# Linear attention and ELU feed-forward on one core: one matmul slice and one VectorE sum reordered at the end of the kernel

## The chip, the core and the metric

The kernel runs on one core of a Trainium2 chip. The core has a matrix engine (TensorE, PE in the profile), two element-wise engines that can read the accumulators in PSUM (VectorE or DVE, ScalarE or ACT), a third one that works on SBUF only here (GpSimd or POOL), and a queue engine that issues most stores (SyncE or SP). Each engine works through its own instructions in the order in which they were written; engines wait for each other by semaphores. The metric is the device time of one execution in microseconds (us); lower is better.

## What is computed

The reference runs a decaying linear attention (4 batches, 8 heads, 768 positions, head size 64) and feeds its output, as 3072 tokens of 512 features, through a feed-forward layer with an ELU:

```python
x = attn_out.transpose(0, 2, 1, 3).reshape(B * S, H * D)   # 3072 x 512
h = x @ w_in                                               # 512 x 2048
g = np.where(h > 0.0, h, alpha * (np.exp(np.minimum(h, 0.0)) - 1.0))
return (g @ w_out).astype(np.float32)                      # 2048 x 512
```

The change lies wholly in the second product, `g @ w_out`, for the last tokens.

## The kernel before

**Tiling.** The 3072 tokens are 24 blocks of 128 (`NG = 24`). Blocks 0 to 3 go singly, all others in pairs, named by the first block: 4, 6, ... 22. `mm1` computes one eighth of a pair's `h` at a time (8 matmuls into a PSUM tile `psH`); ScalarE then makes `e = exp(h)` (line 680) and the positive part of `h` in place (line 681). The ELU itself, `g = min(e - 1, max(h, 0))`, is one VectorE operation in `flush` (line 640): it is issued not with its own `mm1`, but by the next `flush`, that is at the beginning of the next `mm1` or of the next step of the second product. `pending` holds what has not been issued yet.

**The second product of the pairs 8 to 22** (`SEVEN`) is done by `mm2_seven` (from line 522) as seven products in place of eight: two blocks of tokens, two halves of the hidden features (`f`) and two halves of the output columns (left `L_`, right `R_`, 256 wide) make a 2 x 2 by 2 x 2 product, and sums of blocks are multiplied. `mm2_seven(g0, i)` issues product m = 3, 4, 5, 2, 1, 7, 6 for i = 0 to 6. Each product is `NFT // 2` = 8 slices, one matmul each (line 551), and slice s reads the g tile `gg` of index s // 2, half s % 2. So slice 7 of a product needs the very last g of its pair, and slices 0 to 6 don't. Products 3 and 4 multiply g itself, 5 and 2 the row sums `fp` (VectorE, line 500), 1 the sums `fe`, 7 and 6 the differences `fd`; for pair 22, `fe` and `fd` are made by GpSimd (line 497, `SHARED[22] = 'ED'`).

**Banks.** A pair uses two PSUM banks of 512 columns. `bank0` takes m3 and, added onto it, m5 in the left half, then m1 and, added onto it, m6 in the right half. `bank1` takes m4 and, added onto it, m2 on the left, and m7 on the right. There are two such banks in all (`sides`); the next pair takes the same two the other way round, so `bank1` of pair 22 is the bank in which m1 and m6 of pair 20 were summed.

**What is read out of the banks**, in order: `keep` copies m3 and m4 to SBUF (ScalarE, line 558), GpSimd adds them to `t` (line 594); `corner` copies m3 + m5 and m4 + m2 to the output tiles `osb` (ScalarE, line 569); GpSimd forms `u = t - corner 0` (line 605) and `s2 = t - corner 1` (written over `t`, line 565); VectorE adds m1 to `u` (also line 565) and then forms the two remaining corners from `u` with m7 and from `s2` with m6 + m1 (line 582, "corner sums" below). The corner sums are not issued at once: `last_of` puts them into the list `later`, and `flush` issues them at its end, behind a g that it has just issued and behind one of the row sums (`slow`) that follow from it. Steps 0 and 1 of `mm2_seven` also empty `later` before they take a bank (lines 530 to 534):

```python
        if i < 2:
            while later:
                later.pop(0)[1]()
            z[f"bank{i}"] = ps.tile(
                [128, DM], FP32, tag=f"psM{sides[i]}", name=f"psM{g0 + i}", bufs=1
            )
```

**Order at the end.** A list of steps is written out by the planner (lines 814 to 823): one step of the second product behind each `mm1` while there are `mm1` left, the rest after them. The last steps are: `mm1` of pair 22 (j = 6), step 5 of pair 20 (m7), `mm1` of pair 22 (j = 7, the last), step 6 of pair 20 (m6), then steps 0 to 6 of pair 22 with nothing between them. In that order, step 6 of pair 20 begins with a `flush`, which issues the last g of pair 22 and its row sum `fp`; the corner sum on m6 of pair 20 is issued at the start of step 0 of pair 22.

**Stores.** Both blocks of pair 20 are stored as a whole (256 KB each), those of pair 22 in four quarters (128 KB), by SP in the order in which they were put on the list `stores` (line 624).

Of the kernel before, what the change touches and what calls it, by code (L numbers as in the profile page):

```python
# [15 lines left out]
def kernel(  # L16
# [11 lines left out]
    nc = tc.nc  # L28
# [7 lines left out]
    NFT = DFF // 128  # L36
    NCB = S // L
    NG = B * NCB
# [22 lines left out]
    LAGU = 13  # L61
    LATE = 4
    MACT = 12
    DELAY = 0
    COMB = nc.gpsimd

# [44 lines left out]
    for w in RAW.split():  # L111
        x = {"q": q, "k": k}[w[0]]
        g0 = int(w[1:])
        raw[w] = asb.tile([128, H, 64], FP32, name=f"raw_{w}", tag=f"raw_{w}")
        (nc.sync if w[0] == "q" else nc.scalar).dma_start(
            out=raw[w][:], in_=x[g0, :, 0:L].rearrange("h p d -> p h d")
# [16 lines left out]
    wi16, wo16, wi_of, wo_of = [], [], {}, {}  # L133
# [67 lines left out]
    def zero_st1(b):  # L201
# [21 lines left out]
        out=ident16[:], in0=row[:], scalar1=pos[:, 0:1], scalar2=None, op0=ALU.is_equal  # L223
    )
    nc.vector.tensor_scalar(
        out=causT[:], in0=row[:], scalar1=pos[:, 0:1], scalar2=None, op0=ALU.is_ge
# [143 lines left out]
    def att_M(g):  # L370
# [9 lines left out]
        stt[g] = tmp  # L380
        if g >= MACT:
            for hp in range(NHP):
# [98 lines left out]
    g2, forms, wf, C_done, seven, slow = {}, {}, {}, set(), {}, []  # L481

    def sums(g0, jj):
        t = g2[(g0, jj)]
        p = msb.tile([128, 2, 2, 128], FP16, tag="g", bufs=24, name=f"fp{g0}_{jj}")
        d = msb.tile([128, 2, 2, 128], FP16, tag="g", bufs=24, name=f"fd{g0}_{jj}")
        e = msb.tile([128, 2, 128], FP16, tag="g", bufs=24, name=f"fe{g0}_{jj}")
        forms[(g0, jj)] = (p, d, e)
        ring["n"] += 3
        todo = []  # L490
        for w, out, in0, in1, op in (
            ("P", p, t[:, :, 0], t[:, :, 1], ALU.add),
            ("E", e, t[:, :, 0, 0], t[:, :, 1, 1], ALU.add),
            ("D", d, t[:, :, :, 1], t[:, :, :, 0], ALU.subtract),
        ):
            if w in SHARED.get(g0, ""):
                nc.gpsimd.tensor_tensor(out=out[:], in0=in0, in1=in1, op=op)  # L497
            else:
                todo.append(
                    lambda out=out, in0=in0, in1=in1, op=op: nc.vector.tensor_tensor(  # L500
                        out=out[:], in0=in0, in1=in1, op=op
                    )
                )
        return todo
# [14 lines left out]
    L_, R_ = slice(0, 256), slice(256, 512)  # L519
    later, sides = [], [0, 1]  # L520

    def mm2_seven(g0, i):
        flush()
        while slow and i in (2, 4, 5):
            slow.pop(0)()
        if i == 0:
            seven[g0] = {}
            sides.reverse()
        z = seven[g0]
        while i == 6 and "w1" not in z:  # L530
            late.pop(0)()
# [5 lines that stand above are left out]
            )  # L537
        m = (3, 4, 5, 2, 1, 7, 6)[i]
        half = L_ if i < 4 else R_
        out = z["bank1" if m in (4, 2, 7) else "bank0"][:, half]  # L540
        for s in range(NFT // 2):
            t = g2[(g0, s // 2)]
            p, d, e = forms[(g0, s // 2)]
            u = s % 2
            lhs = {3: t[:, u, 0, 0, :], 4: t[:, u, 1, 1, :], 1: e[:, u, :], 7: d[:, u, 1, :],
                   6: d[:, u, 0, :], 5: p[:, u, 0, :], 2: p[:, u, 1, :]}[m]
            if m in (5, 2):
                rhs = wo16[s][:, 1, R_] if m == 5 else wo16[s][:, 0, L_]
            else:
                rhs = wf[s][:, (3, 4, 1, 6, 7).index(m), :]  # L550
            nc.tensor.matmul(  # L551
                out, lhsT=lhs, rhs=rhs, start=(s == 0 and m in (3, 4, 1, 7)),
                stop=(s == NFT // 2 - 1), skip_group_check=True,
            )

        def keep(n):
            z[n] = msb.tile([128, 256], FP32, tag=n, bufs=1, name=f"{n}_{g0}")
            nc.scalar.copy(out=z[n][:], in_=out)  # L558

        def comb(n, x, y, op, eng=COMB):  # L560

            z[n] = z[x]
            if eng is nc.vector:
                y = out
            eng.tensor_tensor(out=z[n][:], in0=z[x][:], in1=y, op=op)

        def corner(c, half):
            z[c] = msb.tile([128, DM], FP32, tag="osb512", bufs=4, name=f"osb{g0 + c}")
            nc.scalar.copy(out=z[c][:, half], in_=out)
            if last:  # L570
                store(c, half)

        last = g0 == NG - 2

        def store(c, cols):
            cb, b = divmod(g0 + c, B)
            t0 = b * S + cb * L
            stores.append((out_dram[t0 : t0 + 128, cols], z[c][:, cols]))

        def last_of(c, half, x, op):  # L580
            def one():
                nc.vector.tensor_tensor(out=z[c][:, half], in0=z[x][:], in1=out, op=op)  # L582
                store(c, half if last else slice(0, DM))
                C_done.add(g0 + c)

            later.append([DELAY, one])


        if m == 3:
            keep("m3")  # L590
        elif m == 4:
            keep("m4")
            z["t"] = msb.tile([128, 256], FP32, tag="t", bufs=1, name=f"t_{g0}")
            nc.gpsimd.tensor_tensor(  # L594
                out=z["t"][:], in0=z["m3"][:], in1=z["m4"][:], op=ALU.add
            )
        elif m == 5:
            corner(0, R_)
            z["u"] = msb.tile([128, 256], FP32, tag="u", bufs=1, name=f"u_{g0}")
            if COMB is nc.vector:  # L600
                late.insert(0, lambda: nc.vector.tensor_tensor(
                    out=z["u"][:], in0=z["t"][:], in1=out, op=ALU.subtract
                ))
            else:
                nc.gpsimd.tensor_tensor(
                    out=z["u"][:], in0=z["t"][:], in1=z[0][:, R_], op=ALU.subtract
                )
        elif m == 2:
            corner(1, L_)
            if COMB is nc.vector:  # L610
                late.insert(0, lambda: comb("s2", "t", None, ALU.subtract))
            else:
                comb("s2", "t", z[1][:, L_], ALU.subtract)
        elif m == 1:
            late.insert(0, lambda: comb("w1", "u", None, ALU.add, nc.vector))
        elif m == 7:
            last_of(0, L_, "w1", ALU.subtract)
        else:
            last_of(1, R_, "s2", ALU.add)
# [6 lines left out]
    def flush():  # L626
        while pending:
            g0, j, e, r = pending.pop(0)
            n = GSIZE[g0]
            if g0 in SEVEN:  # L630
                if j % 2 == 0:
                    g2[(g0, j // 2)] = msb.tile(
                        [128, 2, 2, 2, 128], FP16, tag="g2", bufs=8, name=f"gg{g0}_{j}"
                    )
                g = g2[(g0, j // 2)][:, j % 2]
            else:
                g = msb.tile(
                    [128, FB // n, n, 128], FP16, tag="g", bufs=24, name=f"g{g0}_{j}"
                )[:]
            nc.vector.scalar_tensor_tensor(  # L640
                out=g.rearrange("p f c t -> p (f c t)"), in0=e[:], scalar=-1.0, in1=r[:],
                op0=ALU.add, op1=ALU.min,
            )
            for f in range(FB // n):
                for c in range(n):
                    gts[(g0 + c, j * (FB // n) + f)] = g[:, f, c, :]
            if g0 in SEVEN and j % 2 == 1:
                slow.extend(sums(g0, j // 2))
        if late:
            late.pop(0)()  # L650
        if slow and len(late) < 2:
            slow.pop(0)()
        for x in later:
            x[0] -= 1
        while later and later[0][0] <= 0:
            later.pop(0)[1]()
# [136 lines left out]
    for g in range(0, NG, 2):  # L793
        u = place[(GFIRST[g], 0)] - (8 if GSIZE[GFIRST[g]] == 4 and g == GFIRST[g] else 0)
# [19 lines left out]
    for x, (g, j) in enumerate(m1):  # L814
        u = first + x
# [3 lines left out]
        n = 2 if back > LAGU and m2[0][0][0] == "2" else 1  # L819
# [44 lines left out]
```

## Time and profile before

| what | value |
|---|---|
| median of 6 runs | 214.51 us (213.37 to 215.1) |
| profiled execution, its own time | 214.35 us |
| span in its profile | 212.6 us |
| mean granted TensorE clock | 0.997 of full speed |
| TensorE matmuls: sum of busy time, number | 197.0 us, 2224 |
| matmuls of the second product of pairs (line 551), busy | 49.7 us in three groups of 128 (16.8, 16.5, 16.4) |
| TensorE idle ahead of its two waiting matmuls at the end | 0.32 us (for a g) and 0.50 us (for a corner sum) |
| last corner sum, start | 209.29 us |

The span runs from the first to the last instruction of the profiled execution; the time of the execution holds some 1.75 us more. In a timeline each line has the start, the length, the engine, the line of the kernel, the operation, what it writes and reads, the shape, how many of them were merged, and in brackets the idle time of the engine ahead of it with what ended it. The length of a matmul row holds the time in which the last matmul drains, so rows overlap; a sequence of matmuls is read by the starts. The chain of waits is followed back from the last instruction: at each step to what released it, or to the instruction before it on its engine.

### The profile page before, as it was taken

To read this page: it belongs to the slowest core of one execution; us is meant where nothing else is said; L and a number is where in the kernel's file an instruction comes from. 1 tells how busy PE (TensorE), PEld (TensorE's weight loads), DVE (VectorE), ACT (ScalarE), POOL (GpSimd) and SP (SyncE) were. 2 spreads that over 40 slices of the span, in tenths; PEclk is the share of its full clock that TensorE was granted. 3 is DMA by queue.
4 is the path that set the end of the run, shared out by engine and by line. 5 is a ranking of instruction groups with operands and counts; after the bars stand their busy time and mean duration, and the time that the engine had idled before them with its cause. 6 is when DMAs were issued, how large, how long until landed. Compare 5 with 4: busy or idle time off the path is not lost.

```text
span 212.6 us, 5654 instructions
## 1 busy us (share of the span) xinstructions
PE 197.0 (93%) x2224; PEld 157.8 (74%) x2224; DVE 159.0 (75%) x294; ACT 138.0 (65%) x277; POOL 159.9 (75%) x187
## 2 busy tenths in 40 slices
PE   0679999999999999999999999999999999999983
PEld 0458776767676775757887887888988888888862
DVE  3864472589956878899879879879989889885522
ACT  4535764874877675866966967867667667577630
POOL 7999699999999999497999999996361201206961
PEclk9999999999999999999999999999999999999998
DMA  8999999999992030999969969979999611011032
GB/s 91 137 164 185 195 189 186 160 186 185 161 152 76 3 99 4 135 160 150 133 89 160 119 81 158 154 52 153 144 89 172 101 52 49 3 49 49 3 117 80
DMA packets 102122, 24.61 MB, mean 116 GB/s; under 512 B 92624, under 2 KB 99280, under 8 KB 102096
## 3 DMA queue, kind: packets, MB, share of 16 engines
q0 software_dynamic: 79760, 13.50, 82.7%
q1 hardware_dynamic: 22336, 10.76, 26.7%
q8 instruction: 17, 0.28, 0.6%
q14 instruction: 9, 0.07, 0.2%
HBM read 27.27 MB, written 6.29 MB: 158 GB/s over the span
## 4 chain that ended last, share of the span: by engine, by line
PE 74%; ACT 7%; DVE 6%; DMA 6%; POOL 3%; issue 1%; SPq 0%; ACTq 0%; POOLq 0%; DVEq 0%
PE psH L674 34%; PE psM L551 21%; PE psM L699 11%; DMA wi<-in_moe_w_in_dram 3%; ACT e L680 3%; ACT psH L681 3%; PE psS L304 3%; DVE gg L640 2%; PE psO L340 2%; DMA kT<-kn 2%; DVE g L640 2%; PE psO L346 2%; POOL kn L107 1%; PE psT L285 1%; POOL qn L107 1%
## 5 line engine op out<-in xcount | busy, mean ns | idle before, releaser
L674 PE MATMUL psH<-xt,wi 128*128 128x256 f16 (+1 forms) x896 | 101.1, 261 | 3.0 <-DVE gg L640 1.6
L674 PEld LDWEIGHTS <-wi 128*128 128x128 f16 x896 | 79.0, 100 | 18.3 <-issue 4.2
L680 ACT ACTIVATE e<-psH 128x512 f32<-128x512 f32 x96 | 57.3, 597 | 48.2 <-PE psH L674 47.3
L681 ACT ACTIVATE psH<-psH 128x512 f32<-128x512 f32 x96 | 56.9, 593 | 0.0
L640 DVE SCALAR_TENSOR_TENSOR gg<-e,psH 128x512 f16<-128x512 f32 x64 | 43.7, 682 | 16.5 <-ACT psH L681 16.2
L640 DVE SCALAR_TENSOR_TENSOR g<-e,psH 128x512 f16<-128x512 f32 x32 | 21.9, 684 | 17.4 <-ACT psH L681 17.2
L320 DVE TENSOR_TENSOR pp<-psS,mask 128x512 f16<-128x512 f32 x48 | 31.4, 683 | 3.9 <-PE psS L304 3.9
L699 PE MATMUL psM<-wo,g 128*128 128x512 f16 x128 | 32.0, 379 | 0.0
L176 POOL TENSOR_TENSOR kd<-kn,ks 128x512 f16<-128x512 f16 x20 | 21.0, 1052 | 5.0 <-DMA kn<-in_k_dram 5.0
L497 POOL TENSOR_TENSOR fd<-gg 128x512 f16<-128x512 f16 x20 | 24.3, 1217 | 0.1
L517 POOL TENSOR_TENSOR wf<-wo 128x256 f16<-128x256 f16 (+1 forms) x28 | 21.1, 791 | 0.2
L497 POOL TENSOR_TENSOR fe<-gg 128x256 f16<-128x256 f16 x16 | 11.7, 734 | 12.2 <-DVE gg L640 10.9
L594 POOL TENSOR_TENSOR t<-m,m 128x256 f32<-128x256 f32 x8 | 5.9, 737 | 18.3 <-ACT m L558 18.3
L699 PEld LDWEIGHTS <-g 128*128 128x128 f16 x128 | 11.7, 98 | 9.6 <-issue 0.2
L551 PE MATMUL psM<-wf,gg 128*128 128x256 f16 x128 | 16.8, 273 | 0.8 <-DVE osb L582 0.5
L551 PE MATMUL psM<-wo,fp 128*128 128x256 f16 x128 | 16.5, 273 | 0.0
L551 PE MATMUL psM<-wf,fd 128*128 128x256 f16 x128 | 16.4, 273 | 0.0
L107 POOL DMA_DIRECT2D qn<-in_q_dram x13 | 14.8, 1137 | 0.9 <-POOLq L848 0.8
L107 POOL DMA_DIRECT2D kn<-in_k_dram x14 | 15.4, 1099 | 0.0
L107 POOL DMA_DIRECT2D vn<-in_v_dram x14 | 15.3, 1100 | 0.0
L500 DVE TENSOR_TENSOR fp<-gg 128x512 f16<-128x512 f16 x32 | 14.4, 451 | 0.6
L551 PEld LDWEIGHTS <-gg 128*128 128x128 f16 x128 | 12.0, 98 | 3.2 <-issue 0.7
(62 smaller groups left out, 249.8 us busy)
## 6 DMA issues: line engine op xcount, KB each, us to landing
out_dram<-osb SPq DMA_DIRECT2D x22, 256.0 KB, 2.7
kn<-in_k_dram POOLq DMA_DIRECT2D x10, 256.0 KB, 6.2
qn<-in_q_dram POOLq DMA_DIRECT2D x10, 256.0 KB, 5.8
vn<-in_v_dram POOLq DMA_DIRECT2D x10, 256.0 KB, 8.7
wi<-in_moe_w_in_dram POOLq DMA_DIRECT2D x8, 256.0 KB, 8.5
wo<-in_moe_w_out_dram POOLq DMA_DIRECT2D x8, 256.0 KB, 8.9
kn<-in_k_dram POOLq DMA_DIRECT2D x4, 128.0 KB, 4.3
vn<-in_v_dram POOLq DMA_DIRECT2D x4, 128.0 KB, 5.6
```

The source lines that it names most:

```text
L107: nc.gpsimd.dma_start(out=t[:].rearrange("p b h d -> p (b h) d"), in_=src)
L176: nc.gpsimd.tensor_tensor(out=kd[:], in0=of(kg, g), in1=ks[:].unsqueeze(2).broadcast_to([128, H, 64]), op=ALU.mult,)
L320: nc.vector.tensor_tensor(out=P[:], in0=pts[hh][:], in1=mask[:, hh::2, :], op=ALU.mult)
L497: nc.gpsimd.tensor_tensor(out=out[:], in0=in0, in1=in1, op=op)
L500: lambda out=out, in0=in0, in1=in1, op=op: nc.vector.tensor_tensor(out=out[:], in0=in0, in1=in1, op=op)
L517: eng.tensor_tensor(out=out, in0=in0, in1=in1, op=op)
L551: nc.tensor.matmul(out, lhsT=lhs, rhs=rhs, start=(s == 0 and m in (3, 4, 1, 7)), stop=(s == NFT // 2 - 1), skip_group_check=True,)
L640: nc.vector.scalar_tensor_tensor(out=g.rearrange("p f c t -> p (f c t)"), in0=e[:], scalar=-1.0, in1=r[:], op0=ALU.add, op1=ALU.min,)
L674: nc.tensor.matmul(pH[:, f * n * 128 : (f + 1) * n * 128], lhsT=wi16[i][:, kk, w * 128 : (w + 1) * 128], rhs=xg[g0][:, kk, :], start=(kk = ...
L680: nc.scalar.activation(e[:], pH[:], AF.Exp)
L681: nc.scalar.activation(pH[:], pH[:], AF.Relu)
L699: nc.tensor.matmul(psM[g][:, cols], lhsT=gts[(g, j * FB + f)], rhs=wo16[i][:, w, cols], start=first and f == 0, stop=end and f == FB - 1, ...
```

## The change

For the last pair (`last`, pair 22) and the one before it (`NG - 4`, pair 20) three things are ordered otherwise:

- Step 6 of pair 20 no longer begins with a `flush`. The last g of pair 22 is issued by the `flush` of step 0 of pair 22, and that step first issues what is in `later`, the corner sum on m6 of pair 20. So on VectorE the order becomes corner sum, g, `fp`, in place of g, `fp`, corner sum.
- Step 0 of pair 22 issues only slices 0 to 6 of m3 and returns.
- Step 1 issues slices 0 to 2 of m4 (`SPLIT = 3`), then slice 7 of m3, ScalarE's copy of m3, and slices 3 to 7 of m4.

The matmul loop becomes a function `terms(m, slices)`, `keep` takes the number of the product, and `last` is set at the top; for all other pairs the order of the instructions is the same. The numbers of instructions stay the same on each engine.

```diff
+    SPLIT = 3
...
     def mm2_seven(g0, i):
-        flush()
+        last = g0 == NG - 2
+        if last and i == 0:
+            while later:
+                later.pop(0)[1]()
+        if g0 != NG - 4 or i < 6:
+            flush()
...
-        out = z["bank1" if m in (4, 2, 7) else "bank0"][:, half]
-        for s in range(NFT // 2):
...
+        def place_of(m):
+            return z["bank1" if m in (4, 2, 7) else "bank0"][:, half]
+
+        def keep(m):
+            n = f"m{m}"
             z[n] = msb.tile([128, 256], FP32, tag=n, bufs=1, name=f"{n}_{g0}")
-            nc.scalar.copy(out=z[n][:], in_=out)
+            nc.scalar.copy(out=z[n][:], in_=place_of(m))
+
+        def terms(m, slices):
+            for s in slices:
...
+                nc.tensor.matmul(
+                    place_of(m), lhsT=lhs, rhs=rhs,
+                    start=(s == 0 and m in (3, 4, 1, 7)),
+                    stop=(s == NFT // 2 - 1), skip_group_check=True,
+                )
+
+        end = NFT // 2
+        if last and i == 0:
+            terms(3, range(end - 1))
+            return
+        if last and i == 1:
+            terms(4, range(SPLIT))
+            terms(3, [end - 1])
+            keep(3)
+            terms(4, range(SPLIT, end))
+        else:
+            terms(m, range(end))
+        out = place_of(m)
```

More of the change, by code (lines that the diff above doesn't have):

```diff
@@ L539, in mm2_seven @@
         half = L_ if i < 4 else R_
-        out = z["bank1" if m in (4, 2, 7) else "bank0"][:, half]
-        for s in range(NFT // 2):
[L542 to L554, printed above, removed]
@@ L556, in keep @@
-        def keep(n):
-            z[n] = msb.tile([128, 256], FP32, tag=n, bufs=1, name=f"{n}_{g0}")
-            nc.scalar.copy(out=z[n][:], in_=out)
+        def place_of(m):
+            return z["bank1" if m in (4, 2, 7) else "bank0"][:, half]
+        def keep(m):
+            n = f"m{m}"
+            z[n] = msb.tile([128, 256], FP32, tag=n, bufs=1, name=f"{n}_{g0}")
+            nc.scalar.copy(out=z[n][:], in_=place_of(m))
+        def terms(m, slices):
+            for s in slices:
+                t = g2[(g0, s // 2)]
+                p, d, e = forms[(g0, s // 2)]
+                u = s % 2
+                lhs = {3: t[:, u, 0, 0, :], 4: t[:, u, 1, 1, :], 1: e[:, u, :],
+                       7: d[:, u, 1, :], 6: d[:, u, 0, :], 5: p[:, u, 0, :],
+                       2: p[:, u, 1, :]}[m]
+                if m in (5, 2):
+                    rhs = wo16[s][:, 1, R_] if m == 5 else wo16[s][:, 0, L_]
+                else:
+                    rhs = wf[s][:, (3, 4, 1, 6, 7).index(m), :]
+                nc.tensor.matmul(
[3 more added lines that the diff above has]
+                )
@@ L560, in comb @@
+        end = NFT // 2
[7 more added lines that the diff above has]
+            terms(4, range(SPLIT, end))
+        else:
+            terms(m, range(end))
+        out = place_of(m)
         def comb(n, x, y, op, eng=COMB):
@@ L571, in corner @@
                 store(c, half)
-        last = g0 == NG - 2
         def store(c, cols):
@@ L589, in mm2_seven @@
         if m == 3:
-            keep("m3")
+            keep(3)
         elif m == 4:
-            keep("m4")
+            keep(4)
             z["t"] = msb.tile([128, 256], FP32, tag="t", bufs=1, name=f"t_{g0}")
```

## The prediction

> **What bounds the kernel now.** I read the table of engines first, then the chain of waits over the last stretch, then each engine's timeline from 200 us on, because the diff touches only what the two last pairs of token blocks issue after the last `mm1`.
>
> ```profile
> PE 197.0 (93%) x2224; PEld 157.8 (74%) x2224; DVE 159.0 (75%) x294; ACT 138.0 (65%) x277; POOL 159.9 (75%) x187
> ```
>
> TensorE is busy for 93% of the span, so at the end too only what makes TensorE stand still can be won. The chain of waits (start, length, what) ends so:
>
> ```profile
> 201.15 0.60 ACT e L680
> 201.75 0.50 ACT psH L681
> 202.25 0.02 issue
> 202.27 0.70 DVE gg L640
> 202.97 0.05 issue
> 203.01 0.29 PE psM L551
> 203.31 0.03 issue
> 203.33 0.42 DVE osb L582
> 203.76 0.04 issue
> 203.80 5.41 PE psM L551 x48
> ...
> 209.29 0.42 DVE osb L582
> ```
>
> The reader is to see that from 201.15 to 203.80 the chain is twice off TensorE, with one matmul between, and that from 203.80 on it is TensorE alone up to the last corner sum. The timeline of TensorE gives the stalls:
>
> ```profile
> 200.89 1.04 PE L551 MATMUL psM<-wf,fd 128*128 128x256 f16 x8
> 201.76 0.93 PE L551 MATMUL psM<-wf,gg 128*128 128x256 f16 x7
> 203.01 0.28 PE L551 MATMUL psM<-wf,gg 128*128 128x256 f16 x1 [0.32 <-DVE gg L640]
> 203.80 1.03 PE L551 MATMUL psM<-wf,gg 128*128 128x256 f16 x8 [0.50 <-DVE osb L582]
> 204.67 1.91 PE L551 MATMUL psM<-wo,fp 128*128 128x256 f16 x16
> ```
>
> Row one is m6 of pair 20. Row two is seven slices of m3 of pair 22, row three its eighth, which waits for the last g; row four is m4 of pair 22, which waits until pair 20's last corner sum has left the bank; then m5 and m2. Eight matmuls are issued in 0.87 us (204.67 - 203.80), so one takes 0.109 us; the 1.03 and 1.04 in the rows hold the 0.17 us in which the last one drains. Seven slices from 201.76 are issued by 202.53, and the eighth is issued only at 203.01. VectorE's timeline says why m4 waits:
>
> ```profile
> 186.91 0.41 DVE L565 TENSOR_TENSOR u<-u,psM 128x256 f32<-128x256 f32 x1
> 187.24 0.68 DVE L640 SCALAR_TENSOR_TENSOR gg<-e,psH 128x512 f16<-128x512 f32 x1
> ...
> 202.27 0.69 DVE L640 SCALAR_TENSOR_TENSOR gg<-e,psH 128x512 f16<-128x512 f32 x1 [0.73 <-ACT psH L681]
> 202.99 0.43 DVE L500 TENSOR_TENSOR fp<-gg 128x512 f16<-128x512 f16 x1
> 203.33 0.41 DVE L582 TENSOR_TENSOR osb<-t,psM 128x256 f32<-128x256 f32 x1
> ```
>
> The corner sum that frees the bank stands third in VectorE's queue, behind the last g and its row sum `fp`. Its matmuls were done at 201.93 (200.89 + 1.04), and VectorE idled 0.73 us ahead of the g. So the chain's step from TensorE to `osb` at 203.31 is a coincidence of times; the sum waited for its queue.
>
> **The change part by part.** No instruction is added or removed on any engine: it is the same 16 matmuls for m3 and m4, one ScalarE copy of m3, one corner sum, one g, one `fp`, and the same stores. Three things are moved.
>
> *Corner sum ahead of the g.* It can begin 0.09 after m6's end (the corner sums at 208.42 and 209.29 start 0.08 to 0.09 after their matmuls): 201.93 + 0.09 = 202.02, and ends at 202.43. The g's inputs are ready at 202.27, so now it queues behind the sum. Rows two above show a g 0.33 us after the start of a 0.41 us sum (187.24 - 186.91; its ScalarE input was done at 187.02, so the queue held it). That gives 202.02 + 0.33 = 202.35, the g 0.08 late. Bounds: 0 late if the sum hid wholly in the idle 0.73, 0.16 late if the g waited for the sum's whole 0.41; I take 0.08 as its row is the same pair of operations. Behind the late g stand `fp` (its readers, slices 6 and 7 of m5, come 0.65 after m5's start) and GpSimd's `fe` and `fd`, priced below.
>
> The Trainium skill has a rule against putting the sum in front: in "VectorE: DVE Perf Modes", section "The DRAIN you can't avoid", each operation is followed by a flush of about its duration less 266 ns, during which the next can't start. By it, an estimate from that page, the flush of the 0.41 us sum is 0.15, the g would start at 202.58, and the gain worked out here would shrink by 0.23. The rows at 186.91 and 187.24 speak against it.
>
> *Three slices of m4 ahead of m3's eighth.* m4's bank is free when the sum ends; TensorE went on 0.06 after it in the row at 203.80 (203.33 + 0.41 = 203.74), so here at 202.49, just before TensorE gets there at 202.53. Three slices, 3 x 0.109, last to 202.86. The g runs from 202.35 to 203.04 (0.69), and 0.05 later (202.27 + 0.69 = 202.96 to 203.01) m3's eighth slice starts: 203.09. TensorE idles 0.23 here, and m4's other five slices are issued by 203.09 + 6 x 0.109 = 203.75, or 0.1 later if the eighth slice's own weight load, which starts with it, isn't hidden.
>
> *m3's copy inside m4.* m5 adds onto m3 in the same half of the same bank, so m5's first matmul waits for ScalarE's copy of m3. In the old order all eight slices of m4 lay behind that copy; now five do. Before: eighth slice 203.01, copy from 203.39 to 203.76 (0.38 later, 0.37 long). After: 203.09 + 0.38 = 203.47, copy to 203.84, and TensorE goes on 0.05 after a ScalarE copy (`kT` copy from 55.65 for 0.59, matmul at 56.29): 203.89. This new wait covers the weight-load doubt. Its bound from below is 203.81, with the 0.30 from last matmul to copy seen at m4 and m5 (last issue 205.43, copy 205.74). Queued behind it on TensorE are m5 and all that follows. m4's copy ends about 204.4, ahead of m2 at 204.76, so it costs nothing; uncovered it would cost its 0.37.
>
> *Sum.* m5 started at 204.67 and will at 203.89: a gain of 0.78. What follows has to shift as a whole. GpSimd: `fe` 203.11 to 204.02 (m1 wants it after 205.64), `fd` to 205.13 (m7 wants it after 207.1), then t 205.09 to 205.81 (it starts only 0.23 earlier than before, since `fd` is now in front of it, not m4's copy), u to 206.5, s2 to 207.2. VectorE's sum on m1 comes at 206.78, so u is ready 0.28 ahead, and s2 more than 1 us ahead of the last sum. The last corner sum goes from 209.29 to 208.51. The four quarter stores on SP keep their order and spacing; the store of pair 20's second block is issued at about 202.5 and not 203.8, 0.9 after the one in front (0.33 us of issue), so it collides with nothing. The 2.9 us from the last sum to the end of the span stay.
>
> The profiled execution took 214.35 us, 1.75 outside its span of 212.6. With 0.78 off, span 211.8 and time 213.6; the median of the six runs stands 0.16 higher, so 214.51 - 0.78 = 213.7 (-0.36%).
>
> **Range of the forecast itself.** Least: g 0.16 late and nothing won elsewhere, gain 0.70; with the weight load or one more handover of 0.05 to 0.1 showing, 0.6. Most: g on time and the copy 0.30 behind, m5 at 203.73, gain 0.94. That is 213.6 to 213.9.
>
> **The rivals.**
>
> *The split hides nothing; only the bank wait goes.* If the three slices of m4 don't get in front (bank freed late, since there is only 0.04 between 202.49 and 202.53), all of m4 follows m3's eighth: issued by 203.09 + 9 x 0.109 = 204.07, gain 0.60, 213.9. Against it: even 0.2 late, the slices still fit into the 0.23 of idle.
>
> *GpSimd becomes the bound.* It has 0.28 to spare at u. If t, u or the hand-overs from ScalarE slip by 0.6, the sum on m1 is 0.3 late; m6 needs its bank back (0.14 to spare), so 0.2 to 0.3 of the gain is lost: gain 0.5, 214.0. For it: t, u and s2 run now without gaps. Against: their durations were 0.72 to 0.73 in all six rows.
>
> *The corner sum holds the g: slower.* The sum stands at the head of VectorE's queue and waits for m6 of pair 20, for s2 on GpSimd and for the buffer's former store. Each 0.1 by which it starts late holds the g, and with it m3, m4, all of m5 and the end. Break-even is a start 0.78 after 202.02, at 202.80; if it came at 204.0 the time would be 214.51 + 1.2 = 215.7. Against it: m6 is in front on TensorE without a wait, s2 ended at 199.56, and ScalarE wrote the same buffer at 196.92, so the store was over.
>
> *More than the tail.* Nothing ahead of 201 us is moved, so no case gives over 0.94; a median below 213.4 would be scatter: the six runs reach from 213.37 to 215.1.
>
> **How the numbers follow.** Forecast 0.75, the split hiding nothing 0.10, GpSimd 0.08, slower 0.05, more 0.02. A measurement of this kernel tells about 0.5%, or 1.07 us, from no change. The forecast's 0.36% lies inside that, nearer its lower edge; with a scatter of some 0.3 to 0.4 in a median of six runs of this spread, about a third of its weight falls below 213.44, and a little of the smaller gains: faster 0.26. Slower 0.05 from its rival; the same 0.69. The range takes the 213.6 to 213.9 and the scatter of such a median on both sides, and on the upper one the smaller gains: 212.9 to 214.5.
>
> **What would show it.** Right: in VectorE's timeline the corner sum at about 202.0 ahead of the g at about 202.35; on TensorE ten matmuls in a row, a gap near 0.23, six more, then a gap near 0.14 that ends by ScalarE's copy of m3; m5 at about 203.9, last corner sum about 208.5, span 211.8. Wrong: a g later than 202.6, an m5 that follows m4 without a gap, or a wait for GpSimd ahead of the sum on m1.

## The result and the profile after

| | kernel before | changed kernel |
|---|---|---|
| median | 213.71 us (69 runs, 212.76 to 215.1) | 212.96 us (32 runs, 212.07 to 214.1) |
| ratio to before, 95% interval | | 0.9966 [0.9954, 0.9978] |
| span of the profile | 212.6 us | 212.2 us |
| start of pair 20's m6, in the profile | 200.89 us | 201.27 us |
| from there to the start of pair 22's m5 | 3.78 us | 3.00 us |
| from there to the last corner sum | 8.40 us | 7.63 us |

The changed kernel is 0.34% faster, or 0.73 us of 213.71, with an interval of 0.47 to 0.98 us. That is clear of zero and below the 0.5% named in the prediction.

The two profiles can't be compared by their absolute times: 0.38 us are lost ahead of the changed stretch in the changed kernel's profile (201.27 - 200.89), where both kernels issue the same instructions in the same order. So all that follows is read from the start of pair 20's m6. The chain of waits of the changed kernel from 201 us on (start, length, what), its last 8 pieces:

```profile
201.96 0.45 issue
202.40 0.42 DVE osb L608
202.82 0.61 DVE gg L666
203.43 0.05 issue
203.48 5.34 PE psM L567 x46
208.81 0.04 DVEq L608
208.85 0.04 issue
208.90 0.42 DVE osb L608
```

The chain of before came back to TensorE between the g and the corner sum and left it again; this one leaves it once. The sum is now ahead of the g, and the TensorE piece has 46 matmuls (m3's eighth slice, five slices of m4, and 40 of m5 to m6). The timelines of TensorE and VectorE, of the changed kernel:

```profile
201.27 1.04 PE L567 MATMUL psM<-wf,fd 128*128 128x256 f16 x8
202.15 2.16 PE L567 MATMUL psM<-wf,gg 128*128 128x256 f16 x16
204.27 1.91 PE L567 MATMUL psM<-wo,fp 128*128 128x256 f16 x16
```

```profile
202.40 0.42 DVE L608 TENSOR_TENSOR osb<-t,psM 128x256 f32<-128x256 f32 x1 [0.48 <-POOL fd L498]
202.74 0.68 DVE L666 SCALAR_TENSOR_TENSOR gg<-e,psH 128x512 f16<-128x512 f32 x1
203.45 0.42 DVE L501 TENSOR_TENSOR fp<-gg 128x512 f16<-128x512 f16 x1
...
208.90 0.42 DVE L608 TENSOR_TENSOR osb<-t,psM 128x256 f32<-128x256 f32 x1 [0.45 <-PE psM L567]
```

TensorE's 16 matmuls of m3 and m4 are one row, because each matmul's drain of 0.17 us covers most of a gap; by the starts they take 2.12 us (204.27 - 202.15), where 16 x 0.109 = 1.75 would do. So 0.37 us of standing still is left, against 1.16 in the kernel before (204.67 - 201.76 = 2.91). The weight loads show the first gap, the only one that stands in brackets:

```profile
202.04 1.08 PEld L567 LDWEIGHTS <-gg 128*128 128x128 f16 x10
203.47 0.55 PEld L567 LDWEIGHTS <-gg 128*128 128x128 f16 x6 [0.35 <-DVE gg L666]
```

Ten loads, then the eighth slice's at 203.47, when the g is there. The second gap is the wait for ScalarE's copy of m3:

```profile
203.85 0.37 ACT L553 COPY m<-psM 128x256 f32<-128x256 f32 x1 [1.23 <-PE psM L567]
```

It ends at 204.22, and m5 starts 0.05 later. The corner sum's bracket names GpSimd's `fd`, but that had ended at 201.94, 0.46 before the sum; m6's matmuls ended at 202.31 (201.27 + 1.04), and the sum began 0.09 later.

### The profile page after: what moved, and what is told of

Its sections match the earlier page's. It is cut to its first block, busy times and chain, and to the rows that moved or that the text cites. A ratio compares the mean times of both kernels' runs of the same rounds, so it can differ in the third digit from the quotient of the medians.

```text
span 212.2 us, 5654 instructions
## 1 busy us (share of the span) xinstructions
PE 197.1 (93%) x2224; PEld 157.4 (74%) x2224; DVE 160.0 (75%) x294; ACT 138.0 (65%) x277; POOL 159.8 (75%) x187
## 4 chain that ended last, share of the span: by engine, by line
PE 68%; ACT 9%; DVE 8%; POOL 7%; DMA 3%; issue 3%; ACTq 0%; POOLq 0%; DVEq 0%
PE psH L700 32%; PE psM L567 18%; PE psM L725 10%; ACT e L706 4%; DVE gg L666 4%; ACT psH L707 3%; DMA wi<-in_moe_w_in_dram 3%; PE psS L305 3%; PE psO L341 2%; DVE g L666 2%; PE psO L347 1%; POOL fe L498 1%; POOL kn L108 1%; PE psT L286 1%; POOL qn L108 1%
```

## The experiments

All were read by the same two distances from the start of pair 20's m6, which repeat to 0.01 us from profile to profile of one kernel (the two runs of the changed kernel below), while that start itself lay between 199.54 and 201.74 us in the fourteen profiles of this study, although all kernels are the same up to there. Hence the ratios of whole runs, with intervals 0.3 to 0.5% wide for the variants, tell all but e2_split_only from the kernel before (f2_fill4 barely), but not the variants from each other.

| run | m5 after | last corner sum after | ratio to before, 95% interval |
|---|---|---|---|
| kernel before | 3.78 us | 8.40 us | |
| changed kernel | 3.00 | 7.63 | 0.9966 [0.9954, 0.9978] |
| e1_sum_only | 3.19 | 7.82 | 0.9955 [0.993, 0.9981] |
| e2_split_only | 4.02 | 8.64 | 0.9993 [0.997, 1.0016] |
| e3_split5 | 3.01 | 7.63 | 0.9945 [0.9919, 0.997] |
| e4_sum_twice | 3.34 | 7.96 | 0.9959 [0.9933, 0.9986] |
| f1_fill2 | 3.09 | 7.50 | 0.9961 [0.9945, 0.9978] |
| f2_fill4 | 3.09 | 7.46 | 0.9977 [0.9955, 0.9998] |
| f3_fill4_fd | 3.10 | 7.47 | 0.9955 [0.9933, 0.9976] |
| f4_split7 | 3.18 | 7.81 | 0.9958 [0.9938, 0.9978] |
| g1_own7_fd | 3.09 | 7.28 | 0.9956 [0.9937, 0.9976] |
| g2_own7 | 3.09 | 7.36 | 0.9952 [0.9928, 0.9975] |
| h1_after_again | 3.00 | 7.62 | 0.9968 [0.9944, 0.9991] |
| h2_own7_fd_again | 3.09 | 7.28 | 0.9959 [0.9936, 0.9981] |

**One half of the change at a time.** The first keeps the corner sum ahead of the g and issues m3 and m4 whole:

```diff
-        if last and i == 0:
-            terms(3, range(end - 1))
-            return
-        if last and i == 1:
...
-        else:
-            terms(m, range(end))
+        terms(m, range(end))
```

> The corner sum stays ahead of the last g; m3 and m4 are issued whole, one after the other. Measured on TensorE from the start of pair 20's m6 to the start of pair 22's m5: 3.78 us in the kernel before, 3.00 in the changed one. My theory: m3's eighth slice still waits for the g (at 2.20), then all eight slices of m4 follow it, m5 at 3.18, or 3.28 if the eighth slice's own weight load shows: 0.50 to 0.60 of the 0.78 us come from the sum alone, ratio to before 0.9972 to 0.9977. Rival 'the split hides nothing': 3.00, as in the changed kernel. Rival 'the bank wait costs nothing, the split does it all': 3.7 or more.

TensorE's timeline of that run:

```profile
199.71 1.04 PE L567 MATMUL psM<-wf,fd 128*128 128x256 f16 x8
200.58 0.93 PE L567 MATMUL psM<-wf,gg 128*128 128x256 f16 x7
201.91 1.16 PE L567 MATMUL psM<-wf,gg 128*128 128x256 f16 x9 [0.40 <-DVE gg L657]
202.90 1.91 PE L567 MATMUL psM<-wo,fp 128*128 128x256 f16 x16
```

Seven slices, the wait for the g at 2.20 (201.91 - 199.71), then nine in a row: m4 follows without a wait for its bank. m5 is at 3.19, so the sum alone brings 0.59 of the 0.78. The other half alone has the order of before on VectorE:

```diff
     def mm2_seven(g0, i):
         last = g0 == NG - 2
-        if last and i == 0:
-            while later:
-                later.pop(0)[1]()
-        if g0 != NG - 4 or i < 6:
-            flush()
+        flush()
```

> The split stays, the order on VectorE is that of before (g, row sum, corner sum). My theory: the bank comes free 2.85 us after the start of pair 20's m6 as before, m4's first three slices wait for it until 2.91, m3's eighth slice, though its g is long there, is queued behind them until 3.24, its copy ends at 3.91 to 3.99, and m5 starts at 3.96 to 4.04 (before 3.78): 0.2 to 0.26 us slower than before, ratio 1.0009 to 1.0012. Rival 'the split alone gives part of the gain': m5 below 3.78, ratio below 1.

```profile
201.05 0.93 PE L563 MATMUL psM<-wf,gg 128*128 128x256 f16 x7
203.09 1.14 PE L563 MATMUL psM<-wf,gg 128*128 128x256 f16 x9 [1.11 <-DVE osb L604]
204.20 1.91 PE L563 MATMUL psM<-wo,fp 128*128 128x256 f16 x16
```

This is again TensorE's timeline. The g ended at 202.25 on VectorE, yet m3's eighth slice stands in the queue behind three slices of m4, which wait for the corner sum up to 203.09 (2.91 after m6's start). m5 comes at 4.02, 0.24 later than before. So the split by itself loses, as expected; the ratio is too coarse to say so for the whole run (its interval has 1 in it), the tail says it. The rival that the split alone gives part of the gain falls.

**Is it the chain g, eighth slice, copy of m3, m5?** Two other sizes of the split, `SPLIT = 5` and `SPLIT = 7` in place of 3:

> Five slices of m4 ahead of m3's eighth in place of three. My theory: the gap ahead of the eighth slice (0.23 us) goes to near 0, the gap ahead of m5 (0.14) grows to 0.36, and m5 stays at 3.00 us after the start of pair 20's m6, since g, eighth slice, ScalarE's copy and m5 are one chain; time as the changed kernel within 0.05 us. Rival 'the copy of m3 sets nothing, what counts is TensorE work in front of the g': m5 at about 2.78, 0.22 us faster than the changed kernel.

> Seven slices of m4 ahead of m3's eighth. My theory: the eighth slice is now late for its g by TensorE's own queue (starts at 2.42 us after the start of pair 20's m6 in place of 2.20), so its copy and m5 are 0.2 us later than in the changed kernel: m5 at 3.12 to 3.2. Rival 'the order of the slices doesn't matter once no gap is left ahead of the g': m5 at 3.00 or earlier.

TensorE with five slices ahead, then with seven:

```profile
201.63 1.94 PE L567 MATMUL psM<-wf,gg 128*128 128x256 f16 x16
203.76 1.91 PE L567 MATMUL psM<-wo,fp 128*128 128x256 f16 x16 [0.19 <-ACT m L553]
```

```profile
200.78 1.91 PE L567 MATMUL psM<-wf,gg 128*128 128x256 f16 x16
203.09 1.91 PE L567 MATMUL psM<-wo,fp 128*128 128x256 f16 x16 [0.41 <-ACT m L553]
```

With five, the sixteen matmuls have no visible gap and m5 waits for ScalarE's copy of m3 in place of them: 3.01, no gain. With seven, the eighth slice has fourteen matmuls in front of it and comes 0.2 too late (200.78 + 14 x 0.109 = 202.31, which is 2.40 after m6's start in place of 2.20), and m5 with it, at 3.18. The stall moves, and m5 keeps to the chain. Next, one more corner sum was put ahead of the g:

```diff
             def one():
+                if g0 == NG - 4 and c == 1:
+                    x2 = msb.tile([128, 256], FP32, tag="x2", bufs=1, name="x2")
+                    nc.vector.tensor_tensor(out=x2[:], in0=z[x][:], in1=out, op=op)
```

> The corner sum ahead of the g is done twice, the first time into a tile that nothing reads. My theory: the g starts one hand-over of VectorE's queue later, 0.33 us, and everything to the end with it: m5 at 3.33 us after the start of pair 20's m6, last corner sum 0.33 later, 0.45 us of the gain over before left. Rival 'the g has slack and GpSimd's chain or the stores set the end': end unchanged. Rival 'a flush follows each operation on VectorE': 0.5 or more later per operation.

VectorE's timeline:

```profile
201.47 0.42 DVE L610 TENSOR_TENSOR x<-t,psM 128x256 f32<-128x256 f32 x1 [0.49 <-PE psM L567]
201.81 0.41 DVE L611 TENSOR_TENSOR osb<-t,psM 128x256 f32<-128x256 f32 x1
202.14 0.68 DVE L669 SCALAR_TENSOR_TENSOR gg<-e,psH 128x512 f16<-128x512 f32 x1
```

Each sum holds what is behind it for 0.33 to 0.34 us, less than its own 0.41, and m5 and the last corner sum are 0.34 and 0.33 later. The g has no slack, the end follows it one to one, and neither GpSimd nor the stores absorb any of it. Here the first sum's bracket names TensorE.

**Taking the rest of the stalls away.** By then the tail had 0.37 us of idle TensorE left. m1 needs neither the last g nor m3's copy for its first slices, but its half bank shares a bank with m3 and m5. In these runs it gets one of the two `psH` banks, and its first `FILL` slices go between m4 and m5:

```diff
+    FILL = 2
...
         def place_of(m):
+            if last and m in (1, 6):
+                return z["own"][:, 0:256]
             return z["bank1" if m in (4, 2, 7) else "bank0"][:, half]
...
             terms(4, range(SPLIT, end))
+            z["own"] = ps.tile([128, FB * 128], FP32, tag="psH", bufs=2, name="own")
+            terms(1, range(FILL))
+        elif last and m == 1:
+            terms(1, range(FILL, end))
```

> As the changed kernel, but pair 22's m1 (with m6 added onto it) goes into one of the two psH banks, idle by then, and its first two slices are issued between m4 and m5. My theory: they cover TensorE's 0.14 us wait for ScalarE's copy of m3; m5 starts at 3.08 us after the start of pair 20's m6 (3.00 in the changed kernel) with two slices less behind it, so the last corner sum comes 0.14 us earlier than in the changed kernel. Rival 'the wait for the copy is not what holds m5': last corner sum unchanged or later.

The last corner sum came 0.13 earlier than in the changed kernel (7.50): m5 had waited 0.14 for the copy. Now the two slices of m1 stand in that place, and m5 follows them 0.21 after their start, without a gap:

```profile
202.42 0.38 PE L570 MATMUL own<-wf,fe 128*128 128x256 f16 x2
202.63 1.91 PE L570 MATMUL psM<-wo,fp 128*128 128x256 f16 x16
```

With `SPLIT = 5` and `FILL = 4`:

> Five slices of m4 ahead of m3's eighth and four slices of m1 (own bank) between m4 and m5, so that TensorE has no gap left between pair 20's m6 and m5. My theory: m5 at 3.08 us after the start of pair 20's m6 with four slices less behind it; TensorE alone would end 0.36 us earlier than in the changed kernel, but GpSimd's u (with its own fd in front of it) then ends behind m1, the sum on m1 waits for it, and m6 or the sum on m7 with it: 0.15 to 0.3 us earlier at the last corner sum. Rival 'GpSimd keeps slack': the full 0.36.

And with the last `fd` on VectorE:

```diff
-            if w in SHARED.get(g0, ""):
+            if w in ("E" if (g0, jj) == (NG - 2, 3) else SHARED.get(g0, "")):
```

> As the run with four slices of m1 in front, and the last fd is made by VectorE, idle at that time, in place of GpSimd. My theory: GpSimd's t, u and s2 come some 0.4 us or more ahead of need, TensorE runs without a gap to the end, last corner sum 0.36 us earlier than in the changed kernel, about 1.14 us ahead of the kernel before: ratio 0.9945 to 0.995. Rival 'GpSimd wasn't in the way': same end as the run without this edit.

Both ended at about the same place, 7.46 and 7.47. The first was within its range, but not for the reason given, as the second shows: it missed its 0.36 by 0.2, so GpSimd was not what was missing. TensorE and then ScalarE in the run with `fd` on VectorE:

```profile
205.35 0.60 PE L570 MATMUL own<-wf,fe 128*128 128x256 f16 x4
205.98 1.03 PE L570 MATMUL psM<-wf,fd 128*128 128x256 f16 x8
```

```profile
205.55 0.37 ACT L604 COPY osb<-psM 128x256 f32<-128x256 f32 x1 [0.50 <-PE psM L570]
```

m1's four slices are issued by 205.79 (205.35 + 4 x 0.109), m7 starts at 205.98, 0.06 after ScalarE's copy of corner 1 (205.92). That copy reads the left half of the bank of which m7 writes the right; with eight slices of m1 in between it had always been over. I had not counted this wait. To test it, m7 got the second `psH` bank:

```diff
-            if last and m in (1, 6):
-                return z["own"][:, 0:256]
+            if last and m in (1, 6, 7):
+                return z["own7" if m == 7 else "own"][:, 0:256]
...
+        elif last and m == 7:
+            z["own7"] = ps.tile([128, FB * 128], FP32, tag="psH", bufs=2, name="own7")
+            terms(7, range(end))
```

> As the run with four slices of m1 in front and the last fd on VectorE, and m7 of pair 22 goes into the second psH bank. My theory: there m7 waited 0.19 us for ScalarE's copy of corner 1, which reads the other half of m7's bank; in a bank of its own it follows m1 without a gap. From the start of pair 20's m6: m7 at 5.28 us (5.47 with the wait), last corner sum at 7.27 (7.63 in the changed kernel, 8.40 before): 1.13 us less than before, ratio 0.9945 to 0.995. Rival 'm7 waits for something else (its fd, a matmul record)': m7 stays at 5.47 and the last corner sum at 7.47.

> The same with the last fd on GpSimd as in the changed kernel. My theory: GpSimd's u ends at about 5.7 us after the start of pair 20's m6, the sum on m1 waits for it until 5.76 and ends at 6.18, m6 needs it and starts at 6.23 in place of 6.15: last corner sum at about 7.35, 0.08 us later than with fd on VectorE. Rival 'GpSimd wasn't in the way': 7.27, no difference.

TensorE and VectorE with `fd` on VectorE:

```profile
205.38 0.60 PE L570 MATMUL own<-wf,fe 128*128 128x256 f16 x4
205.81 1.91 PE L570 MATMUL own<-wf,fd 128*128 128x256 f16 x16
...
206.08 0.42 DVE L603 TENSOR_TENSOR u<-u,own 128x256 f32<-128x256 f32 x1 [2.13 <-PE own L570]
...
207.82 0.42 DVE L618 TENSOR_TENSOR osb<-t,own 128x256 f32<-128x256 f32 x1 [0.51 <-PE own L570]
```

VectorE with `fd` on GpSimd:

```profile
206.59 0.42 DVE L603 TENSOR_TENSOR u<-u,own 128x256 f32<-128x256 f32 x1 [3.15 <-POOL u L641]
...
208.19 0.42 DVE L618 TENSOR_TENSOR osb<-t,own 128x256 f32<-128x256 f32 x1 [0.60 <-PE own L570]
```

In its own bank m7 follows m1 without a gap (205.81 is 5.27 after m6's start), and the last corner sum is at 7.28, as worked out. With `fd` on GpSimd the sum on m1 waits for `u`, and the end is 0.08 later, also as worked out. So GpSimd does become the next thing in the way, but only when TensorE has no gap left; with m7's wait in place it had been hidden.

**The changed kernel and the shortest tail, side by side.**

> The changed kernel once more, beside the fastest variant on the same chip. My theory: last corner sum 7.63 us after the start of pair 20's m6 as in its first profile (the tail repeats to 0.02 us); median 0.77 us under that of before. Rival 'the 0.78 was a chance of one profile': another value of the tail by more than 0.05.

> The variant without gaps in the tail once more. My theory: last corner sum at 7.28 us after the start of pair 20's m6, median 0.35 us under that of the changed kernel run beside it and 1.12 under before; with a scatter of some 0.5 us per run and 12 runs each, the difference to the changed kernel may well not be told from nothing. Rival 'the gain in the tail is given back elsewhere': median not under the changed kernel's although its tail is shorter.

The tails repeat: 7.62 and 7.28. The medians were 213.00 and 212.64 us beside 213.67 for the kernel before. Over its two runs the shortest tail has a mean of 212.61 us (24 runs), the changed kernel 212.99 (its 32 runs) and 212.98 (the 12 here): 0.38 less, where the tails differ by 0.34 to 0.35. With a standard deviation of 0.53 us per run the standard error of the difference is 0.53 x sqrt(1/24 + 1/44) = 0.13. But these runs come from different chips, and on that of g1_own7_fd the kernel before was faster too (median 213.28, here 213.67). On the one chip where both ran, the means are 212.98 and 212.75 us (12 runs each): 0.23 less, with a standard error of 0.23. So the shortest tail is shown to be faster than the kernel before (both its intervals lie below 1); that the whole time is also shorter than that of the changed kernel is likely, but not shown. For the tail it is shown.

## Why the prediction was right

The place, the mechanism and the size held. Shifted by the 0.38 us by which m6 began later, the terms are:

| step of the prediction | predicted | measured |
|---|---|---|
| corner sum starts | 202.02 + 0.38 = 202.40 | 202.40 |
| g starts, behind it | 202.35 + 0.38 = 202.73 | 202.74 |
| m3's eighth slice | 203.09 + 0.38 = 203.47 | 203.47 (weight load) |
| idle on TensorE, both gaps | 0.23 + 0.14 = 0.37 | 2.12 - 1.75 = 0.37 |
| m5 starts | 203.89 + 0.38 = 204.27 | 204.27 |
| last corner sum | 208.51 + 0.38 = 208.89 | 208.90 |
| gain in the tail | 0.78 | 0.78 at m5, 0.77 at the last sum |
| gain in the median | 0.78 | 0.75 (213.71 - 212.96) |

*The sum of the parts.* Of the 0.78, the sum alone gives 0.59, the split on top of it 0.19; the split without the sum costs 0.24. The prediction's 0.60 for "only the bank wait goes" is what the first of these runs measured, though as a rival for the whole change it was wrong: all three slices did get in front.

*The g held by the sum.* 0.33 by the rows of the kernel before, 0.34 in the changed one, and 0.33 to 0.34 again where the sum was doubled. The wait for a flush behind each operation, which the prediction took from the Trainium skill's "VectorE: DVE Perf Modes", section "The DRAIN you can't avoid", isn't seen in this pair of operations: the g began 0.08 before the end of the sum's row, not 0.15 after it. The same section adds that a next operation that is not held starts earlier; the prediction left that out, so the section is no rule against the sum in front.

*The copy of m3 as a new wait.* Right, and shown twice: with five slices ahead the whole stall stands at the copy, and with two slices of m1 in front of m5 the wait is gone and the end comes 0.13 earlier, against the 0.14 of the prediction.

*GpSimd.* Its t began where it was expected (205.48; 205.09 + 0.38 = 205.47), but u and s2 each began 0.08 after the end of the one before, a hand-over that the prediction left out. So u had 0.16 to spare (ended 207.00, sum on m1 at 207.16) and not 0.28. It cost nothing here, and 0.08 in the variant without other gaps. GpSimd in the changed kernel:

```profile
205.48 0.72 POOL L620 TENSOR_TENSOR t<-m,m 128x256 f32<-128x256 f32 x1
206.28 0.72 POOL L631 TENSOR_TENSOR u<-t,osb 128x256 f32<-128x256 f32 x1
207.08 0.72 POOL L593 TENSOR_TENSOR t<-t,osb 128x256 f32<-128x256 f32 x1
```

*The absolute time.* The stated 213.7 lies 0.74 above the measured 212.96, almost all of it by the level it started from: the six runs shown had a median of 214.51, the 69 of now 213.71. The sum of the tail could not have known that. The median lies outside the 213.6 to 213.9 that were worked out from the tail, and inside the whole range only because that was widened for scatter, 0.06 above its lower end (212.9): that part is luck. The prediction also took 0.5% as the least change that can be told from none; with 69 and 32 runs the interval is only 0.24% wide, and 0.34% is told.

## What to carry to other kernels

Where a matmul waits for its bank, look at what stands in front of the operation that releases the bank, in that operation's own queue: here a 0.41 us sum, ready 0.25 us before the g in front of it, kept a bank 1.3 us longer than it had to (until 203.74, in place of 202.43), and putting it first made the g only 0.09 later (1.47 in place of 1.38 after m6's start). The split of m3 and m4 paid only once the wait for the bank was gone; alone it made the tail longer. And when the last visible stalls are filled, re-check the copies that were hidden by the work that was moved: each of them can become the next wait, one bank or one queue further on.

## What the runs showed that was not expected

The time ahead of the tail, which the kernels have in common, differed by up to 2.2 us between profiles (199.54 to 201.74 at the start of pair 20's m6), three times what the change brings. Of the 2.2 us between the two extremes, f1_fill2 and f2_fill4, 1.65 are there already at early matmuls of the attention part (the second group into `psU`, at 28.70 and 30.35 us); why the first 30 us differ was not tried.

The last `fd` took 0.89 us on VectorE in all three runs in which it was moved there, where the eleven other `fd` of f3_fill4_fd that VectorE makes took 0.41 to 0.42. GpSimd was at work on `fe` beside it; GpSimd and VectorE in that run:

```profile
202.81 0.84 POOL L499 TENSOR_TENSOR fe<-gg 128x256 f16<-128x256 f16 x1 [1.62 <-DVE gg L673]
203.04 0.89 DVE L502 TENSOR_TENSOR fd<-gg 128x512 f16<-128x512 f16 x1
```

The `fd` ended at 203.93, 0.28 after GpSimd's `fe` (203.65). VectorE's own `fe` shows the like. As a rule it took 0.28 us, but in the same run 0.82 at 151.37 and 0.60 at 163.94 and 179.19. Each of these three began while a GpSimd sum was running, and each ended 0.15 after that sum (152.19, 164.54 and 179.79, against 152.04, 164.39 and 179.64). Operations that began ahead of GpSimd's kept their time: the row sum `fp` at 202.70 took its usual 0.42, with GpSimd's `fe` beside it from 202.81, and an `fe` at 148.10 took 0.28, with GpSimd's `t` from 148.16. So in these rows a VectorE operation of this kind that begins while GpSimd's is running ends only a fixed time after it. That it waits for GpSimd fits them all, but was not tested by a run of its own; here 0.89 was still less than GpSimd's 1.15, and off the path.
